# Turning q, k and the attention output with VectorE block transposes and a DRAM buffer instead of TensorE transposes

## The chip, the core and the metric

The kernel runs on one core of a Trainium2 chip. Five engines work side by side, each through its own list of instructions in order: TensorE (PE, matrix products into PSUM), VectorE (DVE), ScalarE (ACT), GpSimd (POOL) and SyncE (SP), which here issues nearly all the transfers between DRAM and the on-chip memory (SBUF). Sixteen DMA engines carry those transfers out. The metric is the device time of one execution in microseconds (us).

## What is computed

The inputs are q, k, v and o_gate of shape (4, 8, 768, 40) (batch, heads, steps, head size), two gates per step and head, and three weight matrices. First an attention with a matrix memory (an mLSTM), step by step for each batch and head:

```python
m_new = np.maximum(f_gate[:, :, t] + m, i_gate[:, :, t])
f_stab = np.exp(f_gate[:, :, t] + m - m_new)
i_stab = np.exp(i_gate[:, :, t] - m_new)
C = f_stab * C + i_stab * np.einsum('bhd,bhe->bhde', vt, kt)
n = f_stab * n + i_stab * kt
h_tilde = np.einsum('bhde,bhe->bhd', C, qt)
denom = np.maximum(np.abs(np.einsum('bhd,bhd->bh', n, qt)), 1.0)
y[:, :, t] = sigmoid(o_gate) * h_tilde / denom
```

Then a gated feed-forward layer over the 3072 tokens, whose input x is y with the heads side by side (320 columns):

```python
out = (sigmoid(x @ w_gate) * (x @ w_val)) @ w_out     # 320 -> 1536 -> 320
```

## The kernel before

**Chunks and units.** The 768 steps are cut into 6 chunks of 128. A unit is one chunk of one batch, so there are 24 units, n = 4 c + b. Within a unit the attention is computed as a matrix of scores (q times k, times a decay matrix d), times v, plus what the state C of the earlier chunks gives. The feed-forward layer (FFN) is cut into 103 steps: each takes one of the 12 slices of 128 hidden columns, for two batches of a chunk (256 tokens) or for all four (512 tokens).

**Names of the steps of a unit n** (a suffix .g is one of three groups of heads, 3, 3 and 2). lq, lk, lv, lo and ld load q, k, v, o_gate and the decay row. tr transposes q and k on TensorE through an identity matrix (line 638 from unit 8 on), six transposes in all. kh, kl and qk (lines 645, 650, 657) copy the result out of PSUM: kh is the part rounded to the format fp32r, kl the remainder, qk a full copy. From unit 8 on, sw (line 672) stores kh and kl into a DRAM buffer, six DMAs, and sr (lines 683 and 686) loads them back in another arrangement, four DMAs: three blocks of 40 rows on top of each other, so that one matmul with 120 rows (s, line 664, one per head) gives the sum of the high and low products. t multiplies the scores by d. da, db, va and vb split d and v, av (line 753) multiplies them, in and ti add the state's part, nd, ns and ro make the output x. xd copies 64 columns of it, xt (line 795) transposes it on TensorE in three pieces, xh and xl (lines 802 and 806) split it into high part and remainder for the FFN. cs, cd, cm and ca update the state. The units 0 to 7 use an older way for the scores, without the DRAM buffer (lines 599 to 629).

**Steps of an FFN step.** u0, u1 and r0, r1 are the products with w_gate and w_val (lines 863, 867, 868), th is the tanh on ScalarE, gx the product on VectorE, gh and gl the split on ScalarE and VectorE, dn (lines 897 to 899) the product with w_out, one per batch. ob stores a finished block of the output. The names that begin with w (wd, wa, wb, ...) load and split the weights.

**The order.** Nothing is planned at run time: a list of some 2,700 names, ORDER, is written out by hand or by a program, and the steps are issued in this order. Each engine thus gets its own instructions in that order and waits in place when an input isn't there; SP's list holds the transfers in the same way, so a transfer that waits holds back the later ones.

**Buffers.** The names in the first argument of sbt are tags: tiles with the same tag take turns in as many buffers as are given (one if none). The operands of the scores (tags bh and bl) have one buffer each, so a unit's sr waits for the last score matmul of the unit before. The PSUM tag pa has two buffers, in which tr, s, in, av, xt and cs take turns. The DRAM buffers are two, one for even and one for odd units.

Of the kernel before, what the change touches and what calls it, by code (L numbers as in the profile page):

```python
# [23 lines left out]
    'AV': 2,  # L24
    'K': [4, 12, 3, 0, 0, 12],
# [11 lines left out]
    i3 lf li wz lk0 i1 wm lq0 wdv0 i2 ga tap tr0.2 tr0.0 lo1 i0 lq1 gm0 sp1.0 cp0.0 cp0.2 sp0.0 i6 gb tac ee1.0  # L37
    tr0.1 sp0.1 i5 gc qb0.0 em1.0 gm1 gm2 gm3 cp0.1 ee0.0 em0.0 ee0.1 em0.1 lk1 tr1.1 tr1.0 wdr0 lk2 gs0 cp1.0 wav0
    war0 wdg0 cp1.1 sp1.1 qb0.2 s0.2 tr1.2 qb1.1 ee1.1 lv0 l10 qb1.0 dl0 t0.2 kw0 cp1.2 lq2 s0.0 qb0.1 wag0 s1.0
    qb1.2 wbv0 s0.1 ld2 t0.0 wbr0 em1.1 zs3 t0.1 wbg0 wcr0 og1 lo0 wcv0 wor0 dl1 lv1 wov0 s1.1 s1.2 wcg0 tr2.0 cp2.0  # L40
    l11 t1.2 whr0 t1.0 av0 lv3 whv0 wdo0 wdo1 og0 t1.1 ns0 cs0 ee2.1 wlr0 nd0 ro0 av1 wog0 cm0.0 wlv0 wao0 wao1
    tr2.1 wbo0 xd0 cp2.1 wbo1 wco1 qb2.1 whg0 nd1 wdv1 ns1 wco0 cm0.1 xt0 xh0 ro1 ld3 qb2.0 woo0 xd1 lq3 woo1 ee2.0
    xt1 xl0 wdg1 lo2 lo3 who0 wlg0 xh1 xl1 u0.0 gm4 gm5 r0.0 who1 ee3.1 wlo1 u1.0 th0 wdo2 kw1 r1.0 cs1 wlo0 wag1
    wbg1 og3 tr2.2 gs1 wao2 wdr1 lq5 lv2 wav1 l12 gx0 gh0 cm1.0 cm1.1 wcg1 zs1 gl0 wbv1 wog1 wbo2 gd whg1 em2 wco2
    lk3 ld4 dl2 kw2 u0.1 u1.1 tr3.0 wdg2 cp2.2 tr3.2 lv5 qb2.2 cp3.0 tr3.1 cp3.2 og2 cp3.1 qb3.0 wlg1 s2.1 s2.0 woo2
    who2 tab t2.1 r0.1 wlo2 war1 wag2 l13 zs0 t2.0 tbp tbc lk4 r1.1 dn0.1 qb3.1 wcv1 wbr1 zs2 th1 s2.2 t2.2 cs2
    cm2.1 cm2.0 av2 dn0.0 gx1 gh1 wov1 whv1 wlv1 qb3.2 lo6 wcr1 wbg2 tdp wor1 tdc wdo3 u0.2 ld5 wdv2 nd2 wao3 ns2
    tep gl1 dn1.1 s3.1 dn1.0 ro2 xd2 ee3.0 em3 wbo3 u1.2 wco3 whr1 dl3 wlr1 wdr2 woo3 who3 wlo3 tec t3.1 ee4.1 s3.2
# [140 lines left out]
def mlstm_then_gated_ffn_kernel(  # L189
# [101 lines left out]
    if PARAM["V32"] < NCH - 1:  # L291
# [659 lines left out]
```

## Time and profile before

| | |
|---|---|
| time, median of 3 runs | 557.59 us (554.11 to 567.98) |
| profiled execution | 555.66 us, of which 553.7 us are the span from the first to the last instruction |
| busy: TensorE, VectorE, ScalarE, GpSimd | 530.0, 328.0, 230.1, 246.8 us |
| DMA | 131644 packets, 72.34 MB |

In a row that describes a group of instructions stand the line, the engine, the operation, output<-input with sizes, the count, then after the bar the busy time in us and the mean of one in ns, then the idle time of the engine just before them and what ended it. Matmuls overlap, so a busy time summed over groups of TensorE counts the same moment more than once. Rows in order of time begin with the start and the length in us. Rows of transfers issued by SP (SPq) give the time that the issue takes, not the transfer.

### The profile page before, as it was taken

How to read it: one execution, taken by the hardware profiler on the slowest of the kernel's cores; microseconds unless marked ns; L12 is line 12 of the kernel's file. 1: busy time of each engine (PE TensorE's matmuls, PEld its weight loads, DVE VectorE, ACT ScalarE, POOL GpSimd, SP SyncE). 2: the span in 40 equal slices, each digit the busy share in tenths (PEclk: the TensorE clock that was granted, in tenths of full speed). 3: DMA queues.
4: the chain of work that ended last, by engine and by line, in shares of the span. 5: the costliest groups of instructions: out<-in, count | busy, mean ns of one | idle time of the engine just before them, and what ended most of it. 6: DMA issues, size and time to landing. Idle time of an engine off the chain costs nothing.

```text
span 553.7 us, 10954 instructions
## 1 busy us (share of the span) xinstructions
PE 530.0 (96%) x4101; PEld 485.6 (88%) x4101; DVE 328.0 (59%) x734; ACT 230.1 (42%) x580; POOL 246.8 (45%) x293
## 2 busy tenths in 40 slices
PE   7678999999989999999999999999999999999997
PEld 7567988879989899998889887988988888999997
DVE  5988877865655564764564654667543554543332
ACT  4767874663523433343342353233243232233322
POOL 3676646565444633337447381663701574300000
PEclk9879999999999999999999999999999999999999
DMA  9897573430787446277786537667047674010000
GB/s 205 228 234 211 135 225 73 134 106 22 179 194 184 125 113 126 58 178 203 171 200 120 114 118 161 177 168 181 25 133 154 147 183 115 27 26 25 25 1 24
DMA packets 131644, 72.34 MB, mean 131 GB/s; under 512 B 103112, under 2 KB 120776, under 8 KB 131592
## 3 DMA queue, kind: packets, MB, share of 16 engines
q1 hardware_dynamic: 130504, 71.39, 52.4%
q8 instruction: 32, 0.52, 0.4%
q10 hardware_dynamic: 1088, 0.26, 0.3%
q14 instruction: 20, 0.16, 0.1%
HBM read 56.95 MB, written 14.68 MB: 129 GB/s over the span
## 4 chain that ended last, share of the span: by engine, by line
PE 73%; DMA 9%; DVE 7%; ACT 4%; SPq 2%; issue 2%; POOL 1%; ACTq 0%; DVEq 0%; POOLq 0%
PE pg L863 28%; PE po L897 7%; PE po L899 6%; PE po L898 6%; PE pg L867 5%; PE pg L868 5%; PE av L753 4%; DMA qs<-scr 2%; PE s L664 2%; PE in L736 2%; PE pt L638 2%; PE cs L816 2%; DVE gl L887 1%; PE av L760 1%; PE xt L795 1%
## 5 line engine op out<-in xcount | busy, mean ns | idle before, releaser
L863 PE MATMUL pg<-xh,wh 128*128 128x256 f32 (+1 forms) x412 | 106.3, 340 | 2.0 <-ACT sg L873 1.4
L877 DVE SCALAR_TENSOR_TENSOR sg<-sg,pg 128x256 f32<-128x256 f32 (+1 forms) x103 | 54.1, 525 | 89.0 <-PE pg L868 72.9
L863 PE MATMUL pg<-xl,wh 128*128 128x256 f32 (+1 forms) x412 | 101.6, 328 | 0.0
L863 PE MATMUL pg<-xh,wl 128*128 128x256 f32 (+1 forms) x412 | 101.5, 328 | 0.0
L882 ACT ACTIVATE gh<-sg 128x256 fp32r<-128x256 f32 (+1 forms) x103 | 51.8, 502 | 107.2 <-DVE sg L877 80.8
L897 PE MATMUL po<-oh,gh 128*128 128x320 f32 x288 | 95.8, 332 | 0.0
L899 PE MATMUL po<-oh,gl 128*128 128x320 f32 x288 | 89.7, 311 | 1.0 <-DVE gl L887 1.0
L873 ACT ACTIVATE sg<-pg 128x256 f32<-128x256 f32 (+1 forms) x103 | 48.1, 467 | 101.1 <-PE pg L868 61.1
L898 PE MATMUL po<-ol,gh 128*128 128x320 f32 x288 | 89.2, 310 | 0.0
L887 DVE TENSOR_TENSOR gl<-sg,gh 128x256 fp32r<-128x256 f32 (+1 forms) x103 | 67.2, 652 | 36.5 <-ACT gh L882 36.1
L863 PEld LDWEIGHTS pg<-xl,wh 128*128 128x128 f32 x412 | 69.7, 191 | 7.2
L863 PEld LDWEIGHTS pg<-xh,wl 128*128 128x128 f32 x412 | 69.6, 190 | 7.2
L863 PEld LDWEIGHTS pg<-xh,wh 128*128 128x128 f32 x412 | 67.2, 191 | 5.3 <-ACT sg L873 2.3
L867 PE MATMUL pg<-xh,w 128*128 128x256 f32 (+1 forms) x206 | 70.4, 343 | 0.1
L868 PE MATMUL pg<-xl,w 128*128 128x256 f32 (+1 forms) x206 | 67.3, 328 | 0.0
L709 POOL TENSOR_TENSOR dr<-d 128x1024 f32<-128x1024 f32 x16 | 31.7, 1979 | 61.6 <-DVE d L693 61.4
L897 PEld LDWEIGHTS po<-oh,gh 128*128 128x128 f32 x288 | 54.5, 189 | 2.9
L898 PEld LDWEIGHTS po<-ol,gh 128*128 128x128 f32 x288 | 54.4, 189 | 2.9
L899 PEld LDWEIGHTS po<-oh,gl 128*128 128x128 f32 x288 | 54.2, 188 | 1.7 <-DVE gl L887 1.7
L693 DVE TENSOR_TENSOR d<-s,d 128x384 f32<-128x384 f32 (+1 forms) x72 | 35.5, 508 | 28.1 <-PE s L664 22.2
L593 POOL TENSOR_SCALAR_AFFINE_SELECT d<-d 128x1024 f32<-128x1024 f32 x22 | 25.8, 1175 | 45.7 <-ACT d L589 44.9
L585 POOL TENSOR_TENSOR d<-at,d 128x1024 f32<-128x1024 f32 x16 | 31.8, 1995 | 26.7 <-DMA d<-mscr 19.1
(143 smaller groups left out, 916.5 us busy)
## 6 DMA issues: line engine op xcount, KB each, us to landing
d<-mscr SPq DMA_DIRECT2D x22, 512.0 KB
ks<-scr SPq DMA_DIRECT2D x16, 360.0 KB
qs<-scr SPq DMA_DIRECT2D x16, 360.0 KB
k<-in_k_dram SPq DMA_DIRECT2D x24, 160.0 KB
o<-in_o_gate_dram SPq DMA_DIRECT2D x24, 160.0 KB
v<-in_v_dram SPq DMA_DIRECT2D x24, 160.0 KB
su_o<-in_moe_w_out_dram SPq DMA_DIRECT2D x12, 320.0 KB
out_dram<-ob SPq DMA_DIRECT2D x24, 160.0 KB
```

Source lines behind the costliest of these rows:

```text
L585: E("ea", n).tensor_tensor(dm[n], a, dm[n], ALU.subtract)
L693: nc.vector.tensor_tensor(y, ps_[n, g][:, :nh, :], y, ALU.mult)
L863: nc.tensor.matmul(p, w[y][:, a, fs], x[c][:, a, n0:n1], start=(i + a == 0), stop=False)
L867: nc.tensor.matmul(pg[n, y], w2[y][:, fs], xh[c][:, 2, n0:n1], start=False, stop=False)
L868: nc.tensor.matmul(pg[n, y], w2[y][:, fs], xl[c][:, 2, n0:n1], start=False, stop=True)
L873: nc.scalar.activation(s, pg[n, 0], AF.Tanh, scale=0.5)
L877: nc.vector.scalar_tensor_tensor(sgs[n], sgs[n], 1.0, pg[n, 1], ALU.add, ALU.mult)
L882: nc.scalar.activation(ghs[n][:, :nt], sgs[n], AF.Copy)
L887: E("gl", n).tensor_tensor(gls[n][:, :nt], sgs[n], ghs[n][:, :nt].bitcast(F32), ALU.subtract)
L897: nc.tensor.matmul(p, ghs[n][:, ts], oh[:, j, :], start=(j == 0), stop=False)
L898: nc.tensor.matmul(p, ghs[n][:, ts], ol[:, j, :], start=False, stop=False)
L899: nc.tensor.matmul(p, gls[n][:, ts], oh[:, j, :], start=False, stop=(j == NF - 1))
```

## The change

From chunk 2 on (units 8 to 23, the two new parameters QT and XT) there are no TensorE transposes of q, k and the output.

For q and k: tq turns 32 by 32 blocks of both on VectorE (two instructions, 320 columns each). tw writes the result to a DRAM buffer in runs of 32 numbers (128 bytes), in four DMAs, so that the buffer holds q and k with the head dimension as rows. sr loads it three times each for k and q, on rows 0, 42 and 84 (six DMAs, runs of 512 bytes; 42 rows each, of which 2 belong to the next head and are masked). sh on ScalarE rounds it to fp32r, with the sign turned in the one block that is to hold the remainder; sl on VectorE adds the full number there and nothing elsewhere, so that the operands hold high, remainder, high (k) and high, high, remainder (q), as before. The score matmuls have 126 rows instead of 120, one per head as before. sq loads the plain q for the state's part (two DMAs).

For the output: tx turns blocks on VectorE, xw writes them to DRAM (four DMAs), xr loads the turned output (three DMAs) into a buffer of tag dc, and xh and xl split it from there. xl moves from VectorE to GpSimd, and xd is dropped.

Two new set-up steps, i7 (the masks with signs) and i8 (zeros behind the DRAM buffers), replace zs0 to zs3. ORDER is replaced as a whole: 2,724 names for 2,710. Around the score matmuls of units 20 and 21 the new list reads:

```
... sl20.1 s20.1 s20.2 dn69.2 u0.71 gx70
dn68.0 og21 t20.1 s20.0 sr21.10 t20.0 u1.71 sr21.11 sr21.12 dn69.3 em21 gh70 r1.71 sq20.1 r0.71 gl70 sr21.00
sr21.02 sr21.01 dn69.0 dn70.0 dn70.3 t20.2 th71 gx71 lo22 l120 tq22 dn69.1 dn70.1 sh21.1 u1.72 dn70.2 r1.72
sl21.1 ld22 u0.72 da20 gh71 gl71 dn71.1 dn71.0 sh21.0 r0.72 lv22 th72 sl21.0 dn71.3 gx72 dn71.2 s21.1 s21.2 ...
```

The core of the diff:

```diff
+    'QT': 2,
+    'XT': 2,
...
+    DX = D + 2
+    scq = [dram.tile([2 * DM + 2, L], F32, name=f"scq{n}", tag=f"scq{n}") for n in range(2)]
+    scx = [dram.tile([DM, L], F32, name=f"scx{n}", tag=f"scx{n}") for n in range(2)]
+    rsign = const.tile([P, 6], F32, name="rsign")
...
+        def turned_out(name, dst, src):
+            dv = dst.rearrange("(n j) t -> j n t", j=32)
+            for a in range(4):
+                @op(f"{name}{n}.{a}")
+                def _(a=a):
+                    ts = slice(32 * a, 32 * a + 32)
+                    nc.sync.dma_start(dv[:, :, ts], src()[ts].rearrange("j (n i) -> j n i", i=32))
+
+        if bounced:
+            sc = scq[b % 2]
+
+            @op(f"tq{n}")
+            def _():
+                split[n] = t = sbt("kh", [P, 2, DM], F32, f"tq_{n}")
+                for x, y in enumerate((qt, kt)):
+                    nc.vector.transpose(t[:, x, :], y[n].rearrange("p h d -> p (h d)"))
+
+            turned_out("tw", sc[: 2 * DM], lambda: split[n].rearrange("p x d -> p (x d)"))
+
+            for x, y in ((1, "k"), (0, "q")):
+                for i in range(3):
+                    @op(f"sr{n}.{x}{i}")
+                    def _(x=x, y=y, i=i):
+                        if (n, x) not in stk:
+                            stk[n, x] = sbt("bl" if x == 0 else "bh", [P, 9, L], F32R, f"{y}s_{n}")[:, :H]
+                        src = sc[x * DM : x * DM + DM].rearrange("(h d) t -> d h t", d=D)
+                        src = bass.AP(tensor=src.tensor, offset=src.offset, ap=[[src.ap[0][0], DX]] + [list(z) for z in src.ap[1:]])
+                        nc.sync.dma_start(stk[n, x][i * DX : (i + 1) * DX].bitcast(F32), src)
+
+                @op(f"sh{n}.{x}")
+                def _(x=x, y=y):
+                    r = 3 * DX
+                    sgn[n, x] = t = sbt("st", [P, H, L], F32, f"{y}t_{n}", 3)
+                    nc.scalar.activation(t[:r].bitcast(F32R), stk[n, x][:r].bitcast(F32), AF.Copy, scale=rsign[:r, 5 - x : 6 - x])
+
+                @op(f"sl{n}.{x}")
+                def _(x=x):
+                    r = 3 * DX
+                    R = stk[n, x]
+                    nc.vector.scalar_tensor_tensor(R[:r], R[:r].bitcast(F32), rsign[:r, 3 - x : 4 - x], sgn[n, x][:r], ALU.mult, ALU.add)
+
+            for y in range(2):
+                @op(f"sq{n}.{y}")
+                def _(y=y):
+                    r = 3 * D
+                    if y == 0:
+                        qk[n] = sbt("qk", [P, 3, L], F32, f"qk_{n}", 2)
+                        nc.sync.dma_start(qk[n][:r, :2], sc[: 2 * r].rearrange("(g r) t -> r g t", r=r))
+                    else:
+                        nc.sync.dma_start(qk[n][: 2 * D, 2], sc[2 * r : DM])
+
+            for g, (h0, nh) in enumerate(GROUPS):
+                @op(f"s{n}.{g}")
+                def _(g=g, h0=h0, nh=nh):
+                    ps_[n, g] = p = pst("pa", [P, 3, L], f"s_{n}_{g}")
+                    for m in range(nh):
+                        nc.tensor.matmul(p[:, m, :], stk[n, 1][: 3 * DX, h0 + m, :], stk[n, 0][: 3 * DX, h0 + m, :], start=True, stop=True)
...
+        if xbounced:
+            sx = scx[b % 2]
+
+            @op(f"tx{n}")
+            def _():
+                tx[n] = sbt("kl", [P, DM], F32, f"tx_{n}")
+                nc.vector.transpose(tx[n], xin[n][:, :DM])
+
+            turned_out("xw", sx, lambda: tx[n])
+
+            for y in range(3):
+                @op(f"xr{n}.{y}")
+                def _(y=y):
+                    if n not in xf:
+                        xf[n] = sbt("dc", [P, 3, P], F32, f"xf_{n}", 3)
+                    if y == 0:
+                        nc.sync.dma_start(xf[n][:, :2], sx[: 2 * P].rearrange("(a p) t -> p a t", p=P))
+                    else:
+                        nc.sync.dma_start(xf[n][HP[y - 1], 2], sx[2 * P :])
...
-            nc.scalar.activation(xh[c][:, :, bs], px_[n], AF.Copy)
+            nc.scalar.activation(xh[c][:, :, bs], xf[n], AF.Copy)
...
-            nc.vector.tensor_tensor(xl[c][:, :, bs], px_[n], xh[c][:, :, bs].bitcast(F32), ALU.subtract)
+            (E("xl", n) if xbounced else nc.vector).tensor_tensor(xl[c][:, :, bs], xf[n], xh[c][:, :, bs].bitcast(F32), ALU.subtract)
```

More of the change, by code (lines that the diff above doesn't have):

```diff
@@ new lines @@
+    og15 s15.0 xr13.2 t15.2 sq15.1 s15.1 tw16.2 xw14.1 vb15 t15.0 t15.1 lk17 xr13.1 xl12 dn49.1 da15 xw14.2 gh51
+    gl51 r0.52 dn50.2 th52 av15.0 in15 ti15 dn50.3 tw16.3 dn50.0 db15 r1.52 dn51.3 xw14.3 dn50.1 av15.1 sr16.00
+    av15.2 dn51.0 gx52 gh52 lv16 l116 va16 xh13 ad15 ns15 nd15 ro15 u0.53 xr14.0 tx15 gl52 r0.53 xw15.0 sr16.02
+    xw15.1 u1.53 r1.53 dn52.0 sr16.01 dn51.1 tq17 xr14.1 kw15 xr14.2 xw15.2 tw17.0 xw15.3 dn51.2 th53 gx53 gh53
+    dn52.1 gl53 ea17 u0.54 xl13 xh14 r0.54 dn52.3 dn53.1 ee17 u1.54 r1.54 cs15 dn52.2 dn53.2 dn53.0 dn53.3 sr16.10
@@ L178 @@
+    gh100 gl100 th101 u0.102 r0.102 gx101 u1.102 gh101 gl101 r1.102 dn100.2 dn100.3 dn101.2 dn101.3 th102 gx102
+    gh102 gl102 dn102.3 dn102.2 ob5.3 ob5.2
 """.split()
@@ L334, in _ @@
                                 fill=0.0, base=-(L - 1), channel_multiplier=1)
+    if PARAM["QT"] < NCH:
+        @op("i7")
+        def _():
+            w = rsign[:, 1:4]
+            nc.gpsimd.memset(w, 1.0)
+            nc.gpsimd.affine_select(out=w, in_=w, pattern=[[-DX, 3]], compare_op=ALU.is_ge,
+                                    fill=0.0, base=0, channel_multiplier=1)
+            nc.gpsimd.affine_select(out=w, in_=w, pattern=[[DX, 3]], compare_op=ALU.is_ge,
+                                    fill=0.0, base=D - 1, channel_multiplier=-1)
+            m = rsign[:, 0:1]
+            nc.gpsimd.tensor_tensor(m, w[:, 0:1], w[:, 1:2], ALU.add)
+            nc.gpsimd.tensor_tensor(m, m, w[:, 2:3], ALU.add)
+            nc.gpsimd.tensor_scalar(rsign[:, 4:6], w[:, 1:3], -2.0, m, ALU.mult, ALU.add)
+        @op("i8")
+        def _():
+            for n in range(2):
+                nc.sync.dma_start(scq[n][2 * DM :], warm[:2, :L])
     @op("wm")
@@ L512, in unit @@
         halved = c >= PARAM["AV"]
+        bounced = c >= PARAM["QT"]
+        xbounced = c >= PARAM["XT"]
         spread = n < PARAM["BC"]
@@ L594, in _ @@
                                         fill=0.0, base=0, channel_multiplier=-1)
-        if not stacked:
+        def turned_out(name, dst, src):
[8 more added lines that the diff above has]
+            @op(f"tq{n}")
+            def _():
+                split[n] = t = sbt("kh", [P, 2, DM], F32, f"tq_{n}")
[36 more added lines that the diff above has]
+                        nc.tensor.matmul(p[:, m, :], stk[n, 1][: 3 * DX, h0 + m, :], stk[n, 0][: 3 * DX, h0 + m, :], start=True, stop=True)
+        elif not stacked:
@@ L785, in _ @@
                                      rden[n].unsqueeze(2).broadcast_to([P, H, D]), ALU.mult)
-        @op(f"xd{n}")
-        def _():
-            E("xd", n).tensor_copy(xin[n][:, DM:], xin[n][:, 2 * P : DM])
-        @op(f"xt{n}")
-        def _():
-            px_[n] = p = pst(P_(f"xt{n}"), [P, 3, L], f"xt_{n}")
-            for a in range(3):
-                nc.tensor.transpose(p[:, a, :], xin[n][:, a * P : (a + 1) * P], ident)
+        if xbounced:
+            sx = scx[b % 2]
+            @op(f"tx{n}")
+            def _():
+                tx[n] = sbt("kl", [P, DM], F32, f"tx_{n}")
[10 more added lines that the diff above has]
+                        nc.sync.dma_start(xf[n][HP[y - 1], 2], sx[2 * P :])
+        else:
+            @op(f"xd{n}")
+            def _():
+                E("xd", n).tensor_copy(xin[n][:, DM:], xin[n][:, 2 * P : DM])
+            @op(f"xt{n}")
+            def _():
+                xf[n] = px_[n] = p = pst(P_(f"xt{n}"), [P, 3, L], f"xt_{n}")
+                for a in range(3):
+                    nc.tensor.transpose(p[:, a, :], xin[n][:, a * P : (a + 1) * P], ident)
         @op(f"xh{n}")
```

277 lines of the change are left out of this document (134 added, 143 removed).

## The prediction, made before the change was run

> **What bounds the kernel now.** I read the page first: busy time by engine and the chain that ended last.
>
> ```profile
> PE 530.0 (96%) x4101; PEld 485.6 (88%) x4101; DVE 328.0 (59%) x734; ACT 230.1 (42%) x580; POOL 246.8 (45%) x293
> PE 73%; DMA 9%; DVE 7%; ACT 4%; SPq 2%; issue 2%; POOL 1%; ACTq 0%; DVEq 0%; POOLq 0%
> q1 hardware_dynamic: 130504, 71.39, 52.4%
> ```
>
> TensorE carries the end: 96% busy and 73% of the chain. A busy matmul can hide pipelining, so I asked next for busy time by stage (columns: stretch, length, busy us and instructions by engine, granted clock, DMA share, GB/s) and for TensorE's own waits from 120 us on.
>
> ```profile
> 0.00:56.00 56.00, 44.27 (x267) 37.36 (x268) 44.98 (x105) 36.05 (x105) 33.67 (x54) 0.91 0.91 220
> 56.00:140.00 84.00, 82.89 (x516) 73.28 (x514) 64.74 (x140) 50.39 (x130) 48.60 (x58) 1.00 0.43 116
> 140.00:480.00 340.00, 332.52 (x2735) 304.88 (x2735) 193.00 (x431) 121.61 (x291) 162.26 (x180) 1.00 0.59 143
> 480.00:553.60 73.60, 70.34 (x590) 70.06 (x588) 25.28 (x62) 22.01 (x55) 2.28 (x3) 0.99 0.07 21
> PE s L664 <- DMA qs<-scr: 2.9, 2, 1.8
> PEld s L664 <- issue: 3.5, 2, 2.0
> ```
>
> The change acts from 140 to 480 us. There TensorE is idle 7.5 us of 340, VectorE is busy 57%, ScalarE 36%, GpSimd 48%, and the DMA engines 59%. So work taken off TensorE comes off the time almost in full, provided that the new transfers arrive in time. The 11.7 us that TensorE idles in the first 56 us belong to loading and weight splitting, where DMA (91%) and VectorE (80%) are the full ones.
>
> **TensorE: what goes.** Per unit from 8 on (16 units), six transposes of q and k and three of the output. Their price is the distance between starts, not the 0.27 us that one lasts:
>
> ```profile
> 162.00 0.49 PE L795 MATMUL xt<-ident,x 128*128 128x128 f32 x3
> 162.33 0.27 PE L638 MATMUL pt<-ident,q 128*80 128x128 f32 x1
> ...
> 170.03 0.27 PE L638 MATMUL pt<-ident,q 128*120 128x128 f32 x1
> 170.14 0.27 PE L638 MATMUL pt<-ident,k 128*120 128x128 f32 x1
> 170.25 0.27 PE L638 MATMUL pt<-ident,q 128*120 128x128 f32 x1
> ```
>
> Three output transposes take 0.33 us, and each of the q and k ones 0.11. 16 x 9 x 0.11 = 15.8 us. The score matmuls keep their number and width (126 rows deep for 120), so they cost the same. Four of ten uses per unit of the two rotating PSUM buffers go too; I book nothing for that.
>
> **VectorE, ScalarE, GpSimd.** Rows for what goes and the nearest ones for what comes:
>
> ```profile
> L650 DVE TENSOR_TENSOR kl<-pt,kh 120x256 fp32r<-120x256 f32 x32 | 13.1, 416 | 3.0 <-ACT kh L645 3.0
> L650 DVE TENSOR_TENSOR kl<-pt,kh 80x256 fp32r<-80x256 f32 x16 | 6.6, 412 | 1.3 <-ACT kh L645 1.3
> L657 DVE COPY qk<-pt 120x128 f32<-120x128 f32 x32 | 9.1, 283 | 6.9 <-ACT kh L645 5.8 <-PE in L736 1.1
> L657 DVE COPY qk<-pt 80x128 f32<-80x128 f32 x16 | 4.5, 279 | 2.8 <-ACT kh L645 2.6
> L806 DVE TENSOR_TENSOR xl<-xt,xh 128x384 fp32r<-128x384 f32 x24 | 13.3, 555 | 13.2 <-ACT xh L802 13.1
> L617 DVE COPY qkt<-pt 120x256 f32<-120x256 f32 x7 | 2.9, 419 | 1.4 <-PE pt L606 1.3
> L887 DVE TENSOR_TENSOR gl<-sg,gh 128x256 fp32r<-128x256 f32 x62 | 34.8, 562 | 22.9 <-ACT gh L882 22.6
> L887 DVE TENSOR_TENSOR gl<-sg,gh 128x512 fp32r<-128x512 f32 x41 | 32.3, 788 | 13.6 <-ACT gh L882 13.5
> L645 ACT ACTIVATE kh<-pt 120x256 fp32r<-120x256 f32 x32 | 11.9, 380 | 17.9 <-PE pt L638 16.3 <-DMA scr<-kh 1.6
> L589 ACT ACTIVATE d<-d 128x1024 f32<-128x1024 f32 x16 | 16.8, 1053 | 0.0
> L484 POOL TENSOR_TENSOR ol<-dc_o,oh 128x320 fp32r<-128x320 f32 x12 | 12.3, 1024 | 7.3 <-ACT oh L479 5.6 <-DVE qbd L622 1.7
> L789 POOL COPY x<-x 128x64 f32<-128x64 f32 x23 | 8.4, 364 | 58.2 <-DVE x L784 58.2
> ```
>
> VectorE loses 13.1 + 6.6 + 9.1 + 4.5 + 16 x 0.555 = 42.2 us. It gains 32 sl at 1024 wide: by the slope of the gl rows (0.226 us per 256) 0.788 + 2 x 0.226 = 1.24 us, 39.7 us in all (up to 1.6 each at twice the 512-wide row); and 48 block transposes 320 wide. No transpose stands in the trace; by the copies' slope (0.136 us per 128) 0.49 us each, 23.5 us (between the 512-wide gl's 0.79 and the 128-wide copy's 0.28). Net +21 us, so 214 of some 324: 66%. ScalarE: 32 sh at the 1024-wide row's 1.053 = 33.7, less 48 kh at 0.38 = 18.2, net +15.5, to 42%. GpSimd: 16 xl from the 320-wide row scaled to 384, 1.23 each, less 16 xd at 0.364, net +14, to 54%. All three stay well under TensorE: nothing on the path. If that cover is gone, sl's 1.24 us stand whole ahead of gx and gl in VectorE's order, 1 to 2 us a unit.
>
> **DMA.** Per unit go 160 writes of 3072 bytes, 160 of 1024 and 720 reads of 1536. There come 3840 writes of 128 bytes (tw, xw) and 2720 reads of 512 (sr 2016, sq 320, xr 384). Prices per packet from stretches in which one kind runs alone: the v and k loads (160 bytes), and the last two stores (256 packets of 1280 bytes).
>
> ```profile
> 201.60:204.20 2.60, 2.60 (x24) 2.60 (x23) 1.67 (x5) 1.62 (x7) 0.89 (x3) 1.00 0.89 152
> 548.00:553.60 5.60, 2.34 (x16) 2.07 (x15) 1.14 (x3) 0.85 (x2) 0.00 (x0) 0.93 0.16 59
> 280.00:300.00 20.00, 19.41 (x197) 17.20 (x196) 10.07 (x24) 7.99 (x20) 11.57 (x17) 1.00 0.91 202
> ```
>
> 2.6 us x 0.89 x 16 engines over 395 KB of 160 bytes is 15.0 ns; 5.6 x 0.16 x 16 over 256 is 56 ns. The line through both gives 13.8 ns at 128 bytes, 28 at 512, 47 at 1024, 65 at 1536, 122 at 3072. Goes: 720 x 65 + 160 x 122 + 160 x 47 = 74 engine-us. Comes: 3840 x 13.8 + 2720 x 28 = 129. Net 55 per unit, 55 us of all 16 engines over the kernel; the stage goes from 0.59 x 340 = 201 to 256 us busy in 324, 79%. The run's own mean (52.4% x 553.7 x 16 / 130504 = 35.6 ns at 547 bytes, where the line says 29) would make it 83%. The fullest 20 us of the stage ran at 91%, so this still fits, with less room. Small writes to DRAM are not in the trace: their bounds are the semaphore-sized end of the line, 9 ns, and the 1280-byte store, 56; I take 13.8, being next to the 160-byte row.
>
> The Trainium skill, "DMA: Bandwidth & Descriptors", section Specifications, says that below 512 bytes the engine reads, modifies and writes. Taken as twice the price for the 128-byte writes, its sum is 556 (worked out from rows under the rivals). The 160-byte loads, at 15 ns, show no such step, but they write SBUF; no run here shows so small a write to DRAM.
>
> **Queues and waits.** SP's DMAs per unit go from 10 to 19, at 0.3 to 0.6 us each:
>
> ```profile
> 142.89 1.78 SPq L672 DMA_DIRECT2D scr<-kh  x3
> 150.03 0.33 SPq L683 DMA_DIRECT2D ks<-scr  x1
> 146.18 3.71 DMA scr<-kl
> 151.24 6.74 DMA qs<-scr
> ```
>
> That is 4 us more of a unit's 20 us. New waits on SP: tw on tq, sr on the landing of tw, xr on that of xw; behind them queue the loads of later units and the stores. On ScalarE, sh and xh now wait for transfers, with th and gh behind them; on VectorE sl, with gx and gl behind it.
>
> The tightest loop is the one pair of operand buffers (tags bl, bh): unit n's sr may start only when unit n-1's last score matmul has read them. Before, that was 4 issues (1.6 us) and the landing (6.7): 8.3 us, and the shortest TensorE work that the list put in between was 8.0 (unit 23), hence the 6.4 us of waits quoted first. Now it is 6 issues (2.5), the landing 6.7, one sh 1.05, one sl 1.24: 11.5 us. The work in between, counted in the new list with these prices from the chain:
>
> ```profile
> 256.81 1.40 PE pg L863 x6
> 342.37 0.15 PE po L898
> 343.83 0.23 PE pg L868
> ```
>
> Between the last score matmul of unit 20 and the first of unit 21 stand three u (1.40 each), four r (0.46), eleven dn (0.45): 11.0 us. The same count gives 10.4 for unit 23, 10.8, 11.1, 11.2 and 11.4 for units 17, 19, 22 and 10, and 13 or more elsewhere. Shortfall at 11.5: 3.1 us, where the old loop cost 2.9 as DMA waits: +0.2, and I put +1 for the longer ScalarE and VectorE queues in front of it. The distance from tq to the first score matmul is 25 to 41 us of TensorE work, against some 16 for tw, its 3.7 us landing and the rest: covered.
>
> **First 140 us.** The new list mixes units 2 to 6 earlier into the weight work. Up to u0.12 VectorE's instructions add up to 87 us of work in both lists, and TensorE's to 74 and 75: I book nothing, plus or minus 4. i7 (seven small GpSimd instructions) and i8 (two small stores) come in there, and the four zs stores go: nothing either, under the loading.
>
> **Sum**, against the profiled execution, 555.66 us (span 553.7 and 2.0 around it; the median of the runs shown, 557.59, lies 1.9 above): 555.7 - 15.8 + 1.2 = 541.
>
> **The rivals.**
> *The loop is longer than counted.* Up to four foreign issues stand among sr's six, 1.7 us, and sh may find ScalarE busy: at 14 us instead of 11.5 the shortfall of all units is 19, less the old waits of 2.9: 555.7 - 15.8 + 16 = 556. For it: gaps of 10.4 to 11.4 leave nothing. Against: the old list's shortest gap was equally close to its loop and cost 3.
> *DMA becomes the bound (slower).* Let a 128-byte write cost 2.5 times 13.8 ns, 35, near the run's mean packet. The stage then needs 256 + 1.5 x 53 = 336 us of all engines; at the best sustained share, 91%, it lasts 369 instead of 340: 585. It decides from twice the price on: there 256 + 53 = 309 us, at 91% 340, and the gain is just gone: 556. Against: bytes, not packets, fill most of this traffic, and the 160-byte packets cost 15. (Twice the price is what the rule of the Trainium skill named above would make of it.)
> *More than the transposes goes.* With fewer users of the rotating PSUM buffers the other waits of the stage go, and the first 56 us run better: 531.
>
> **How the numbers follow.** Forecast 53%, its own range 535 to 548; longer loop 17%; twice the price (556) 6%; DMA as the bound 19%; better still 5%. A run of this kernel can be told from no change at about 2%, 11 us: below 544.5 is faster, above 566.8 slower. Of the forecast's 53, 39 lie below 544.5: faster 0.44, same 0.37, slower 0.19. The range 532 to 572 leaves out the better end (4) and most of the DMA case (13).
>
> **What would show it.** Right: TensorE busy near 317 of 324 us in the stage, DMA share near 0.8, score matmuls waiting for sl a few us in all. The longer loop: those waits near 20 us, at units 10, 17, 19, 21 to 23. DMA as the bound: windows at 0.9 over the whole stage, landings far over 7 us, SP issues stretched to several us. Wrong in another way: ScalarE held by sh or xh with th behind it, or a first stage that ends more than 4 us later.

## The result and the profile after

The changed kernel takes 548.02 us (median of 4 runs, 545.87 to 549.6), the kernel before 555.85 us beside it (551.91 to 567.98): a ratio of 0.9865, 95% interval 0.9823 to 0.9907. The ratio leaves out executions in a slower state of the chip, so it isn't quite the quotient of the two medians. That is 1.35% less, between the forecast 541 and no change, and at the upper end of the forecast's own range (535 to 548). The profiled execution took 546.66 us (span 544.9), 9.0 us less than that of before, where the sum had 14.6.

The page of the kernel after: busy time by engine, the main DMA queue, the chain that ended last.

```profile
PE 518.4 (95%) x3957; PEld 472.7 (87%) x3957; DVE 360.5 (66%) x702; ACT 248.0 (46%) x564; POOL 266.2 (49%) x299
...
q1 hardware_dynamic: 221336, 73.20, 62.4%
...
PE 69%; DMA 13%; SPq 6%; DVE 5%; issue 3%; ACT 3%; POOL 1%; ACTq 0%; DVEq 0%; POOLq 0%
```

The 144 transposes are gone (4101 matmuls became 3957). VectorE has 32.5 us more work, ScalarE 17.9, GpSimd 19.4; in the chain, DMA and SP's issues take 19% where they took 11%. Busy time by stage of the kernel after, with the columns of the prediction:

```profile
0.00:56.00 56.00, 44.88 (x256) 36.64 (x257) 44.49 (x107) 36.83 (x109) 33.94 (x56) 0.88 0.85 209
56.00:140.00 84.00, 84.00 (x536) 75.70 (x534) 65.84 (x141) 50.33 (x128) 49.38 (x65) 1.00 0.59 147
140.00:480.00 340.00, 328.06 (x2653) 299.27 (x2652) 227.12 (x402) 141.77 (x280) 180.91 (x178) 0.99 0.71 143
480.00:545.00 65.00, 61.47 (x521) 61.10 (x519) 23.00 (x54) 19.07 (x48) 2.00 (x2) 1.00 0.09 25
```

From 140 to 480 us TensorE now idles 11.9 us instead of 7.5, and the granted clock is 0.99 instead of 1.00. Its own waits after 130 us (waiting line, what it waited for, us in all, times, longest):

```profile
PE pg L967 <- ACT sg L977: 5.6, 5, 2.1
PE s L679 <- issue: 2.8, 1, 2.8
PE s L679 <- PE pg L972: 1.8, 2, 1.0
PE s L679 <- DMA scq<-tq: 0.7, 1, 0.7
```

In the kernel before, the FFN's row (pg), from 120 us on, was:

```profile
PE pg L863 <- ACT sg L873: 1.4, 2, 0.9
```

After 130 us it is one wait of 0.9 us. So the row that grew most is not the score matmuls' (s) but the FFN's, which waited for the tanh (th, line 977). ScalarE's waits between 140 and 480 us show one thing that stood in front of th:

```profile
ACT qt L656 <- DMA qs<-scq: 9.1, 5, 3.9
ACT xh L906 <- DMA xf<-scx: 8.8, 4, 3.0
ACT kt L656 <- DMA ks<-scq: 8.5, 5, 2.9
```

Here ScalarE stands 26.4 us before sh (line 656) and xh (906), for operands that have not landed. The sum alone proves nothing, since before the change ScalarE stood still longer ahead of kh and xh:

```profile
ACT kh L645 <- PE pt L638: 25.5, 22, 3.0
ACT xh L802 <- PE xt L795: 23.7, 12, 5.0
```

But those waits were for TensorE, which was at work meanwhile. A wait for a landing can leave TensorE with nothing to do. The worst place, in order of time (start, length):

```profile
279.31 1.15 ACT L656 ACTIVATE qt<-qs,rsign 126x1024 fp32r<-126x1024 f32 x1 [3.88 <-DMA qs<-scq]
280.37 0.61 ACT L986 ACTIVATE gh<-sg 128x512 fp32r<-128x512 f32 x1
283.39 0.60 ACT L977 ACTIVATE sg<-pg 128x512 f32<-128x512 f32 x1 [2.41 <-DVE gl L991]
...
284.04 0.73 PE L967 MATMUL pg<-xh,wh 128*128 128x512 f32 x2 [2.15 <-ACT sg L977]
```

sh15.0 waits 3.88 us for its load; gh50, which is ready, stands behind it in ScalarE's order. gl50 then finds VectorE in sl15.0 (1.65 us) and two more steps, th51 waits for gl50 since the gate tile sg has one buffer, and TensorE idles 2.15 us. Two stretches around it (busy us by engine, then the granted clock):

```profile
282.00:285.40 3.40, 1.36 (x6) 1.14 (x7) 3.26 (x10) 2.01 (x3) 1.08 (x2) 1.00 0.89 195
285.40:288.80 3.40, 3.40 (x13) 2.79 (x12) 3.11 (x4) 1.52 (x7) 1.60 (x2) 0.51 0.11 41
```

After a stretch of 3.4 us in which TensorE was busy for 1.36 us its clock was granted at half for the next 3.4 us. Outside the first 40 us and the last 2 this never happened in the profiled execution of before.

**Where the gain went.** The end of FFN step 16's tanh came at 135.2 us before and at 134.8 after: the first stage neither gave nor took. From there to the last matmul I take off TensorE's gaps, and half of the time at half clock (matmuls 512 wide start 0.43 us apart there and 0.23 at full clock, so about half the work is lost); what is left is TensorE's own work. All columns are worked out from the traces' records, in us:

| kernel | stretch | gaps | half the time at half clock | left |
|---|---|---|---|---|
| before | 415.2 | 7.5 | 0 | 407.7 |
| after | 406.7 | 11.9 | 1.7 | 393.0 |
| e3, scores twice | 420.8 | 11.4 | 3.4 | 406.0 |
| e1, three moves | 410.8 | 12.8 | 6.8 | 391.2 |
| e2, more moves | 412.6 | 15.2 | 6.8 | 390.5 |
| e5, control of e6 to e8 | 406.0 | 11.0 | 1.7 | 393.2 |
| e6, two operand buffers | 404.4 | 8.4 | 5.1 | 390.8 |
| e7, two gate tiles | 409.5 | 13.1 | 3.4 | 393.0 |
| e8, both | 398.2 | 5.6 | 0 | 392.6 |
| e9, three operand buffers | 428.6 | 27.4 | 12.0 | 389.3 |
| e12, the same without added waits | 399.9 | 6.8 | 0 | 393.1 |

(A gap inside half clock is counted in both columns, so "left" comes out 2 to 4 us low where there is much of both.) TensorE's work fell by 14.7 us, close to the 15.8 booked. Of these, 4.5 went into more gaps and 1.7 into half clock; 0.4 came from the earlier start, and the sum, 8.9, is what the last matmul ends earlier by (541.47 against 550.34). Each row is one execution; those of e5, e8 and e12 are the fastest of their six.

### The profile page after: what moved, and what is told of

It is laid out like the page before. It is cut to its first block, busy times and chain, and to the rows that moved or that the text cites. A ratio compares the mean times of both kernels' runs of the same rounds, so it can differ in the third digit from the quotient of the medians.

```text
span 544.9 us, 10878 instructions
## 1 busy us (share of the span) xinstructions
PE 518.4 (95%) x3957; PEld 472.7 (87%) x3957; DVE 360.5 (66%) x702; ACT 248.0 (46%) x564; POOL 266.2 (49%) x299
## 3 DMA queue, kind: packets, MB, share of 16 engines
q1 hardware_dynamic: 221336, 73.20, 62.4%
## 4 chain that ended last, share of the span: by engine, by line
PE 69%; DMA 13%; SPq 6%; DVE 5%; issue 3%; ACT 3%; POOL 1%; ACTq 0%; DVEq 0%; POOLq 0%
PE pg L967 28%; PE po L1001 6%; PE po L1003 6%; PE po L1002 6%; PE pg L971 5%; PE pg L972 5%; DMA scx<-tx 3%; DMA qs<-scq 3%; PE av L837 2%; PE s L679 2%; DMA d<-mscr 2%; PE s L713 2%; PE av L844 2%; PE in L820 2%; SPq L650 1%
## 5 line engine op out<-in xcount | busy, mean ns | idle before, releaser
L991 DVE TENSOR_TENSOR gl<-sg,gh 128x256 fp32r<-128x256 f32 (+1 forms) x103 | 71.1, 690 | 40.1 <-ACT gh L986 39.8
L1001 PE MATMUL po<-oh,gh 128*128 128x320 f32 x288 | 92.3, 321 | 0.0
L967 PEld LDWEIGHTS pg<-xh,wh 128*128 128x128 f32 x412 | 67.9, 191 | 12.8 <-ACT sg L977 7.7
L971 PE MATMUL pg<-xh,w 128*128 128x256 f32 (+1 forms) x206 | 69.2, 338 | 0.0
L612 POOL TENSOR_TENSOR d<-at,d 128x1024 f32<-128x1024 f32 x16 | 33.0, 2068 | 21.8 <-DMA d<-mscr 17.4
```

Of the source, the lines that this page charges most:

```text
L612: E("ea", n).tensor_tensor(dm[n], a, dm[n], ALU.subtract)
L967: nc.tensor.matmul(p, w[y][:, a, fs], x[c][:, a, n0:n1], start=(i + a == 0), stop=False)
L971: nc.tensor.matmul(pg[n, y], w2[y][:, fs], xh[c][:, 2, n0:n1], start=False, stop=False)
L991: E("gl", n).tensor_tensor(gls[n][:, :nt], sgs[n], ghs[n][:, :nt].bitcast(F32), ALU.subtract)
L1001: nc.tensor.matmul(p, ghs[n][:, ts], oh[:, j, :], start=(j == 0), stop=False)
```

## The experiments

All ratios are to the kernel before, run on the same chip as the experiment. The theory at first (A): matmuls come off one for one, and what is missing went into a few places where a step that waits for a landing operand stands ahead of a step of the gate. Against it (B): the loss is spread, or the round trip through DRAM is the bound.

### e1 and e2: moves in the order list

e1 moves unit 7's denominator behind gl19 and the sign steps of units 13 and 15 behind th45, gl45 and th51. The last of the three:

```diff
-... th50 gx50 sh15.0 dn48.2 dn49.2 sl15.0 dn49.0 ... gl50 th51 lv15 sh15.1
+... th50 gx50 dn48.2 dn49.2 dn49.0 ... gl50 th51 sh15.0 sl15.0 lv15 sh15.1
```

> The changed kernel with three places of the order list mended, in chunks 3 and 4 of the list's first half: the denominator of unit 7 behind gl19, the sign steps sh13.0 and sl13.0 behind th45 and gl45, sh15.0 and sl15.0 behind th51; same instructions, same result. Theory A (the part of the transposes' 15.8 us that did not come off went into a few places where a landing operand's sign step, or a step on VectorE, stands ahead of a gate's step, so that TensorE waits for pg): the gaps of 1.5, 1.4 and 2.2 us at 153, 243 and 284 us go, and with the last of them the half clock that followed (1.7 us): 3 to 6 us less than the changed kernel, ratio to the kernel before about 0.977 to 0.981. Theory B (what is missing is spread: longer loops, slower VectorE steps, a lower granted clock whatever the order): each gap only moves to the next wait, less than 1.5 us comes off, ratio 0.984 to 0.989.

Measured: 548.88 us, ratio 0.9843 (0.9792 to 0.9894), not to be told from the changed kernel's 0.9865. Theory A's 3 to 6 us did not come. In the profile the gap at 243 us is gone and the one at 153 is down to 0.6, but unit 13's scores now wait 1.75 us at 248, and the gap at 284 came back as one of 4.05 us at 289, for gx51, with sl15.0 and the denominator of unit 14 ahead of it on VectorE.

e2 adds moves at units 22 and 23:

```diff
-... gl74 ... sh22.1 ro20 ... tx20 sl22.1 ... sh22.0 sl22.0 th75 gx75 ... t21.0 s22.1 t22.1 s22.0 ... u0.76 r0.76
+... gl74 ... th75 sh22.1 gh75 gx75 ro20 ... tx20 t21.0 sl22.1 ... sh22.0 gl75 sl22.0 ... u0.76 r0.76 u1.76 r1.76 s22.1 t22.1 s22.0
```

> As the run before, and further moves around units 22 and 23: t21.0 ahead of sl22.1, th75, gx75, gh75 and gl75 ahead of the sign steps of unit 22, the matmuls of u0.76 and u1.76 ahead of s22, th78 ahead of sh23.1; same instructions, same result. Theory A: TensorE's gap of 2.75 us ahead of s22 is filled with 2.8 us of matmuls that were ready, and part of the 0.85 us ahead of s23 too: another 2 to 3 us less than the run before, ratio about 0.972 to 0.977, with TensorE's idle time from 135 us on down from 11.9 to about 4 us. Theory B: less than 1 us beyond the run before.

Measured: 553.21 us, ratio 0.9911 (0.9878 to 0.9944): if anything, it took time. The gap ahead of s22 grew from 2.75 to 5.06 us. VectorE's steps there in the profile of e2:

```profile
445.15 0.69 DVE L984 SCALAR_TENSOR_TENSOR sg<-sg,pg 128x512 f32<-128x512 f32 x1 [4.37 <-ACT gh L989]
...
447.18 1.26 DVE L665 SCALAR_TENSOR_TENSOR ks<-ks,rsign,kt 126x1024 fp32r<-126x1024 f32 x1
448.36 2.38 DVE L994 TENSOR_TENSOR gl<-sg,gh 128x512 fp32r<-128x512 f32 x1
450.67 2.91 DVE L665 SCALAR_TENSOR_TENSOR qs<-qs,rsign,qt 126x1024 fp32r<-126x1024 f32 x1
```

The first row shows a slip of mine: gh75 came to stand ahead of gx75, so it rounds the tanh in place of the product (gl75, the difference to the product, makes up for it), and gx75 had to wait 4.37 us for it, with everything behind it on VectorE, sl22.1 too. So e2 does not test the move at unit 22 as it was meant. What it shows besides: gl75 and sl22.0 fell beside two GpSimd steps and took 2.38 and 2.91 us, where they need 0.68 and 1.28 alone (last section), and the idle stretch was followed by 10.2 us at half clock:

```profile
447.30:450.70 3.40, 1.32 (x6) 0.75 (x4) 3.40 (x3) 0.00 (x0) 3.29 (x2) 1.00 0.62 99
450.70:460.90 10.20, 7.21 (x70) 6.96 (x71) 6.72 (x12) 0.60 (x1) 4.20 (x3) 0.50 0.27 76
```

From e1, theory A as I had stated it falls: mending single places shifted the wait to the next step that was late. Whether a clean move at unit 22 would pay stays open. What the late steps share is the landing of the operands, and the next runs go there.

### e3: each score matmul twice

```diff
                         nc.tensor.matmul(p[:, m, :], stk[n, 1][: 3 * DX, h0 + m, :], stk[n, 0][: 3 * DX, h0 + m, :], start=True, stop=True)
+                        nc.tensor.matmul(p[:, m, :], stk[n, 1][: 3 * DX, h0 + m, :], stk[n, 0][: 3 * DX, h0 + m, :], start=True, stop=True)
```

> The changed kernel with each of the 128 stacked score matmuls issued twice into the same place: full result, 128 matmuls of TensorE more, no other work. Theory A (from the second stage on TensorE is the bound, and matmuls come off or on one for one): 128 x about 0.1 us = +12 to +13 us, near 560 us, ratio about 1.008; the operand wait of the next unit starts a microsecond later each time, so it may be 2 us more. Theory B (the operands' round trip through DRAM is the bound from unit 8 on): the second matmuls fall into the time in which TensorE waits and cost 0 to 4 us, ratio under 0.995.

Measured: 559.42 us, ratio 1.0037 (0.9998 to 1.0076), above the changed kernel's 0.9865 by 0.0172, 9.6 us of 557, give or take some 3; the profiled executions differ by 12.3. In the table TensorE's own work rises by 13.0 us, and the gaps hardly change. Theory A holds against theory B's 0 to 4 us: most or all of the added work shows in the time, so most of the 14.7 us that went off TensorE were really to be had.

### e4: each write of turned q and k twice

```diff
...
                     nc.sync.dma_start(dv[:, :, ts], src()[ts].rearrange("j (n i) -> j n i", i=32))
+                    if name == "tw":
+                        sv = spare[n % 2].rearrange("(n j) t -> j n t", j=32)
+                        nc.sync.dma_start(sv[:, :, ts], src()[ts].rearrange("j (n i) -> j n i", i=32))
```

> The changed kernel with each of the 64 writes of turned q and k (128-byte packets) issued a second time into a spare buffer in DRAM: full result, 40,960 packets and 64 issues on SP more. Theory A (DMA at 0.71 of the stage is not the bound): packets at 14 ns over 16 engines are 36 us of DMA time, which raise the share in the stage to about 0.8, and the time by 0 to 5 us, through later issues on SP; ratio 0.985 to 0.996. Theory B (128-byte packets and the queue are what holds the operands up): landings come 2 us later per unit or more, +15 to +36 us, ratio 1.01 to 1.05.

The four runs gave 552.8, 565.5, 566.2 and 568.3 us: too far apart for a ratio, 5 to 20 us above the changed kernel. The stretch from 135 to 540 us of the kernel after and then of e4 (its 566.2 us run), and e4's largest wait of TensorE:

```profile
135.00:540.00 405.00, 393.06 (x3198) 363.84 (x3197) 253.29 (x466) 163.12 (x333) 183.86 (x181) 1.00 0.62 125
```

```profile
135.00:540.00 405.00, 382.56 (x3044) 350.78 (x3042) 248.86 (x451) 156.56 (x317) 180.00 (x181) 0.97 0.69 137
```

```profile
PE pg L971 <- ACT sg L981: 10.8, 7, 2.4
```

The DMA engines are not full: a share of 0.69 with 40,960 packets more. Over the whole span the main queue took 33 us of all sixteen engines more than in the kernel after (66.1% of 564.4 us against 62.4% of 544.9), 13 ns a packet. The times decide nothing: one execution lies 4.8 us above the changed kernel, where theory A put it, and three lie 17 to 20 us above, where theory B put them. The profiled one is of the three; its longer stretch is gaps and half clock (22.4 and 10.2 us in the terms of the table, against 11.9 and 1.7). What the added writes cost by themselves, through packets or through the 64 more issues on SP, stays open.

### e5 to e8: more buffers

The buffers need room in SBUF. In these four kernels the tile of w_out's remainder is the tile of the rounded w_out itself, which therefore counts twice in the result; all instructions and the order stay (the remainder is still computed, into the tile of w_out it came from).

```diff
-    ol = const.tile([P, NF, DM], F32R, name="ol")
+    ol = oh
...
```

```diff
-stk[n, x] = sbt("bl" if x == 0 else "bh", [P, 9, L], F32R, f"{y}s_{n}")[:, :H]        # e6, e8
+stk[n, x] = sbt("bl" if x == 0 else "bh", [P, 9, L], F32R, f"{y}s_{n}", 2)[:, :H]
-sgs[n] = s = sbt("sg", [P, NT], F32, f"sg_{n}")[:, :nt]        # e7, e8
+sgs[n] = s = sbt("sg", [P, NT], F32, f"sg_{n}", 2)[:, :nt]
```

> The changed kernel with the remainder of w_out left out of the result (its tile is the rounded w_out itself), same instructions and order; it frees 15 KB per partition of SBUF and is the control for the next three. Both theories: as the changed kernel, ratio 0.983 to 0.990.

> The control (w_out's remainder left out) with two buffers each for the stacked operands of q and of k, so that SP issues the loads of the next unit without waiting for the last score matmul of this one. Theory A (the loop through the single operand buffers is what TensorE waits for ahead of s, 5.6 us of the changed kernel's 11.9 us of gaps, and what delays the sign steps ahead of th; every window of about 3.4 us with 1.8 us or more idle is followed by half clock, which costs 1.7 us or more): the operands land up to 10 us earlier, the gaps ahead of s fall under 1.5 us, no half clock between 50 and 540 us, 5 to 9 us less than the control, ratio 0.970 to 0.977. Theory B (the gate's chain on VectorE, slowed by GpSimd beside it, is what TensorE waits for, and the s gaps are only where that shows): the gaps move to pg, under 2 us less than the control.

> The control (w_out's remainder left out) with two buffers for the gate tile sg, so that th does not wait for gl of the step before. Theory A: the gaps of pg stay, since they come from sign steps that stand ahead of th and gh in the list; under 2 us less than the control. Theory B: the 5.7 us of gaps ahead of pg go, and the half clock with them: 4 to 7 us less than the control, ratio 0.974 to 0.980.

> The control (w_out's remainder left out) with both: two operand buffers and two gate tiles. If the two are separate causes, the gains of the two runs before add up: gaps from 135 us on near 2 us, no half clock in the middle, 8 to 12 us less than the control, ratio 0.965 to 0.972. If something third holds TensorE up (landing times on the DMA queues, the list itself), it is no better than the better of the two by more than 1.5 us.

| | median us | ratio | 95% interval |
|---|---|---|---|
| e5, control | 548.84 | 0.9837 | 0.9795 to 0.9879 |
| e6, two operand buffers | 542.99 | 0.9726 | 0.9683 to 0.9769 |
| e7, two gate tiles | 549.36 | 0.9846 | 0.9806 to 0.9886 |
| e8, both | 538.71 | 0.9662 | 0.9624 to 0.9701 |

The control stands where the changed kernel stands. Two operand buffers take 5.9 us off it, the size that theory A gave. Where the loop was tight it went as theory A said: SP issues the first load of k 18.8 and 20.0 us ahead of the first score matmul of units 21 and 22 (10.8 and 13.4 in the control), and the waits ahead of the scores of units 22 and 23 fell from 3.0 us to 0.4. But those of units 13 to 15 rose from 2.0 to 4.8; the longest, 2.8 us at unit 14, follows a sl14.0 that took 2.91 us beside a step of GpSimd (last section). So the gaps ahead of s are 5.3 us in all (5.1 in the control), those ahead of pg fell from 5.1 to 2.9, and the half clock that theory A excluded still came (10.2 us). The two traces explain only 3.2 us of the 5.9: the control's is the fastest of its six executions, e6's the second slowest. Two gate tiles alone give nothing, but together with two operand buffers they do: e8 is 10.1 us under the control, and its profile has no half clock between 40 us and the last matmul. TensorE's waits after 130 us, in e6 and then in e8:

```profile
PE s L679 <- issue: 3.6, 3, 2.8
PE pg L967 <- ACT sg L977: 2.8, 3, 1.5
PE s L679 <- ACT sg L977: 1.5, 1, 1.5
```

```profile
PE pg L967 <- DVE sg L981: 1.9, 1, 1.9
PE pg L967 <- ACT sg L977: 1.9, 3, 0.9
PE s L679 <- PE pg L972: 1.4, 2, 0.9
```

The three times fit this reading, which no run shows step by step: the late operands come first, and the gate's single tile passes on what is left of them. With both, 5.6 us of gaps remain, less than the 7.5 of before, and the stretch of the table is 17.0 us shorter than before: TensorE's work came off it in full.

### e9 to e11: the cure in the room that there is

e9 computes everything. Three buffers take turns for the two operands; tx goes to t1 and bmask into the second gate tile's place:

```diff
-stk[n, x] = sbt("bl" if x == 0 else "bh", [P, 9, L], F32R, f"{y}s_{n}")[:, :H]
+stk[n, x] = sb.tile([P, H, L], F32R, tag=turn3(), name=f"{y}s_{n}")     # bl0, bh0, kl0 in turn
...
-tx[n] = sbt("kl", [P, DM], F32, f"tx_{n}")
+tx[n] = sbt("t1", [P, DM], F32, f"tx_{n}", 2)
...
-sgs[n] = s = sbt("sg", [P, NT], F32, f"sg_{n}")[:, :nt]
+sgs[n] = s = sb.tile([P, NT], F32, tag=f"sg{n % 2 if n >= 24 else 0}", name=f"sg_{n}")[:, :nt]
...
-qt[n] = sbt("q", [P, H, D], F32, f"q_{n}", 3)
+qt[n] = sbt("q", [P, H, D], F32, f"q_{n}", 2)
```

> The full computation with both cures in the room that SBUF has: the stacked operands take turns in three buffers in place of two (the third is the tile that tx had; tx goes into t1), the gate tile has two buffers from step 24 on (the second in the place of bmask), q has two buffers in place of three, and seven loads of q stand later in the list for that. Theory A (two separate causes, each to be cured by a buffer, as the runs with more room had it: -1.1% and, both, -1.75%): with one operand of two loaded early, half to all of that: 4 to 9 us less than the changed kernel, ratio 0.968 to 0.977, gaps from 135 us on of 6 to 9 us. Theory B (the second operand still waits for the last score matmul, and both are needed): no gain from the operands, ratio 0.982 to 0.988.

Measured: 570.28 us, ratio 1.0215 (1.0179 to 1.0251), against both theories. The waits of TensorE, of SP (from 100 to 160 us) and of VectorE (from 200 to 250) in e9's profile:

```profile
PE po L1008 <- ACT gh L993: 10.4, 2, 9.9
PE av L844 <- DVE t L832: 5.9, 2, 4.2
```

```profile
SPq L657 <- PE s L720: 16.4, 1, 16.4
```

```profile
DVE t L832 <- DMA scx<-tx: 10.6, 2, 6.5
```

The buffer that my turn gave to unit 8 first was still held by unit 7. SP stood 16.4 us before that load, with the load of o_gate behind it, for which ScalarE waited 13 us ahead of gh. And ti waited for the DMA that reads tx out of t1. Two added waits cost more than the buffers gave.

e10 is e9 with e1's three moves.

> The run before with the three places of the order list mended as in the first run (unit 7's denominator behind gl19, the sign steps of units 13 and 15 behind th45 and th51). Theory A: with the operands early, the sign steps' places no longer decide; within 1.5 us of the run before. Theory B (in the first run the moves only shifted the wait onto operands that were late; with those early the moves are worth the gaps they remove): 2 to 4 us less than the run before.

Measured: 570.79 us, ratio 1.0209 (1.016 to 1.0259): as e9, and as theory A said, though under e9's own waits this says little.

e11 is e9 with xl on VectorE:

```diff
-        'gl': 'v', 'ca': 'v',
+        'gl': 'v', 'xl': 'v', 'ca': 'v',
```

> The kernel with three operand buffers and two gate tiles, and the 16 remainders xl of units 8 to 23 on VectorE (about 0.5 us each) in place of GpSimd (1.09 us each): VectorE takes 8 us more, GpSimd 17 us less. Theory C (GpSimd at work beside VectorE is what lengthens VectorE's steps: sl 1.28 us alone and 1.57 us beside it, gl 0.68 and 1.06 us): the other VectorE steps together take about 6 us less, and the time falls by 1 to 3 us. Theory D (GpSimd's remaining steps lie beside them all the same): VectorE's busy time rises by the whole 8 us, time unchanged or up to 3 us longer.

Measured: 578.58 us, ratio 1.0369 (1.0316 to 1.0422), 8.3 us more than e9. VectorE's busy time rises by 6.6 us, GpSimd's falls by 18.3. Two rows of its VectorE steps:

```profile
L917 DVE TENSOR_TENSOR xl<-xf,xh 128x384 fp32r<-128x384 f32 x16 | 11.3, 707 | 2.9 <-ACT xh L913 1.9 <-DMA scq<-tq 0.9
...
L998 DVE TENSOR_TENSOR gl<-sg,gh 128x512 fp32r<-128x512 f32 x41 | 39.8, 972 | 20.0 <-ACT gh L993 20.0
```

The other VectorE steps together take 4.7 us less (366.1 - 11.3 against 359.5), near the 6 of theory C; sl became 0.08 to 0.09 us shorter, but the 512-wide gl 0.10 longer (0.874 in e9). The time rose all the same, by more than theory D said: TensorE now waits 5.2 us for xl itself ahead of pg, and 3.5 us ahead of dn for gl, where e9 has 0.2.

### e12: the same cure without the added waits

```diff
+        return ("bh0", "bl0", "kl0")[n % 3]
...
+            if xbounced:
+                E("ro", n).tensor_tensor(ot[n], ot[n], rden[n].unsqueeze(2).broadcast_to([P, H, D]), ALU.mult)
+                return
...
-                tx[n] = sbt("kl", [P, DM], F32, f"tx_{n}")
+                tx[n] = sbt("x", [P, DM], F32, f"tx_{n}")
...
-            sgs[n] = s = sbt("sg", [P, NT], F32, f"sg_{n}")[:, :nt]
+            sgs[n] = s = sb.tile([P, NT], F32, tag="q2" if n >= 24 and n % 2 else "sg0", name=f"sg_{n}")[:, :nt]
```

The gate's second tile is the buffer that q gives up after unit 8.

> The full computation with the two cures as in the run of three operand buffers, but without that run's new waits (TensorE stood 9.9 us at 151 us, behind gh, while SP waited 16.4 us in the load of unit 8 for a score matmul of unit 7; and 4.2 us at 239 us, where VectorE's ti waited for the DMA that reads tx, now in t1): the stacked operands begin with the buffer that is free first (bh, then bl, then the former kl), tx lies in x, since the output is scaled in place, the masks bmask and cmask take no room, and q keeps three buffers until unit 8; four loads of q stand later in the list. Theory A (the two cures hold, the loss was the added waits): gaps from 135 us on of 6 to 10 us, at most one stretch of half clock in the middle, 2 to 8 us less than the changed kernel, ratio 0.970 to 0.983. Theory B (with three buffers the second operand still waits, so that only more room helps): ratio 0.984 to 0.990.

Measured: 543.31 us, ratio 0.9769 (0.9724 to 0.9815), whose interval lies wholly below the changed kernel's: the fastest kernel here that computes everything, 2.3% under the kernel before. Theory A holds, though the gain over the changed kernel, 0.0096 of the ratio, is about half of what e8 had under its control (0.0175). Its page's first row and TensorE's waits after 130 us:

```profile
PE 517.0 (96%) x3957; PEld 471.4 (88%) x3957; DVE 356.9 (66%) x702; ACT 247.3 (46%) x564; POOL 265.3 (49%) x296
```

```profile
PE pg L977 <- ACT sg L987: 1.9, 2, 1.6
PE s L686 <- issue: 1.4, 2, 0.9
PE pg L977 <- DVE sg L991: 1.1, 1, 1.1
```

The gaps are 6.8 us, and no half clock falls into the stretch of its profiled execution.

## Where the prediction held, and where it was off

**What goes off TensorE: right.** 15.8 us were booked; the traces give 14.7, and e3 gives 13.0 us for 128 matmuls (0.10 each). TensorE did bound the kernel: in e8, where the new waits are nearly gone, the stretch is shorter by the whole of the work that went.

**The other engines' work: direction right, size too small on VectorE.** +32.5 us against +21. Rows of the kernel after:

```profile
L662 DVE SCALAR_TENSOR_TENSOR ks<-ks,rsign,kt 126x1024 fp32r<-126x1024 f32 x16 | 23.9, 1491 | 6.9 <-ACT kt L656 5.6 <-DMA scq<-tq 1.2
L662 DVE SCALAR_TENSOR_TENSOR qs<-qs,rsign,qt 126x1024 fp32r<-126x1024 f32 x16 | 21.5, 1346 | 10.0 <-ACT qt L656 10.0
L877 DVE STREAM_TRANSPOSE tx<-x 128x320 f32<-128x320 f32 x16 | 8.1, 507 | 0.3
L991 DVE TENSOR_TENSOR gl<-sg,gh 128x512 fp32r<-128x512 f32 x41 | 36.9, 901 | 17.6 <-ACT gh L986 17.6
```

The transposes are at 0.49 to 0.51 us where the copies' slope gave 0.49. sl takes 1.35 to 1.49 us, not 1.24: the estimate holds for a sl alone (1.28 us) and not beside GpSimd (last section). The existing 512-wide gl went from 788 to 901 ns for the same reason, which the sum did not have. ScalarE's +17.9 and GpSimd's +19.4 were booked as 15.5 and 14.

**DMA: not the bound; the sum right, partly by luck.** The share of the stage is 0.71, not 0.79. Over the whole span the main queue took 50 us of all sixteen engines more (62.4% of 544.9 us against 52.4% of 553.7), where 55 were booked, but some 13 of them fell between 56 and 140 us (0.59 against 0.43). In the trace's packet records a 128-byte packet takes 14.0 ns on average, where the line gave 13.8. The larger ones were priced too low on both sides, and that cancelled: a 512-byte packet takes 38 ns, not 28, and the 1536-byte ones that went had taken 104, not 65. So the slower rival falls, at its own point of decision: the price of these writes did not double. The rule of the Trainium skill ("DMA: Bandwidth & Descriptors", Specifications: below 512 bytes read, modify, write), taken as twice the price, gave 556; the section names no price, and these writes of 128 bytes to DRAM show no doubled one. e4 adds that the engines have room.

**The loop: about as long as counted, set against an old cost that was misread.** From the last score matmul of one unit to the first of the next the trace has 11.4, 11.1, 11.6, 11.0 and 11.3 us at units 10, 17, 19, 21 and 23, where I counted a loop of 11.5, and 14.0 at unit 22, the size of the longer-loop rival. At units 10, 17 and 21 TensorE waits 0.1 us or less there, so these distances are its own work and show only that the loop isn't longer. The waits at the six units come to 3.9 us (2.75 at unit 22) for a counted 3.1. From this I took off 2.9 us as the cost of the old loop, and that was wrong: in the trace of before these two waits stand at unit 8 (1.76 us) and at unit 16 (1.11 us, 38 us after the scores of unit 15), and at unit 23, where the old loop was tight, TensorE doesn't wait. (The 6.4 us count these two waits twice, on the matmuls and on the weight loads.) Another 1.7 us stand at units 13 and 14, 16 us behind the unit before, where no shortfall was counted. In all, TensorE's gaps ahead of s grew from 3.4 us to 5.6, +2.2 for the +1.2 that stood for them.

**The term that was mis-sized: the new waits, +1.2 us.** They came to +4.5 us of gaps and 1.7 of half clock. I had counted only the loop that ends in s. The other way of a late operand was named under what would make the prediction wrong, but not priced: ScalarE held by sh or xh with th behind it. It came so: gaps ahead of pg rose from 0.9 to 5.7 us. e6 and e8 show that second buffers for the operands take most of this away (5.9 us, and 10.1 with the gate's second tile), and e1 that the three places in the list which looked guilty were not the cause. I priced neither the passing on through sg nor the clock.

**First 140 us: nothing, as booked** (134.8 against 135.2 us). The rival by which more than the transposes goes did not come: the other waits of the stage (cs, xt, po and the like) did fall, from 3.2 us to 0.5, but pg and s rose by more.

## What to carry to other kernels

When a result that was made on the spot begins to come through DRAM, price its lateness for every step that is queued behind the waiting one, on each engine, not only for the step that reads it. Before moving steps in a list that is full, ask which single buffer makes the transfer start late: a second buffer for it was worth 6 us where three moves in the list were worth nothing that could be measured. A new buffer order brings its own waits: look whether the first tile in turn is free, and what stands behind the transfer that waits for it.

## What the runs showed of the hardware

**TensorE's clock falls after half a window of idling.** The granted clock changes on a grid of 3.41 us. Over all profiled executions of this case there are 1550 windows of this grid between 130 and 520 us that began at full clock; 31 were followed by half clock. Every window with 1.81 us or more of TensorE idle was (25 of 25); between 1.49 and 1.80 us it was 6 of 14; below that, none. Half clock lasts 3.4 us, or 6.8 to 13.7 where gaps go on (10.2 in e2). So gaps that gather in one window cost 1.7 us beyond themselves, while the 7.5 us of before, spread over the stretch, drew no half clock. The Trainium skill ("TensorE: Matmul & The Clock Gate", Part 1: The HAM clock gate) has the window of about 3.4 us and gives an idle window as the condition; here about half of one was enough.

**VectorE steps with two tensors from SBUF grow beside GpSimd, transposes don't.** In the kernel after, sl takes 1.28 us where no GpSimd step overlaps it (17 of 32) and 1.57 on average where one does (up to 2.51); the 512-wide gl 0.68 (17 of 41) and 1.06 (up to 2.43). The transposes of q and k take 0.485 us either way, and gx, 512 wide with one input from PSUM, 0.68. It depends on the step of GpSimd too: where one step covered a sl or gl for over 0.8 of its length, in all runs with the change, xl made it 2.7 times as long on average (11 cases), while the masking of d on line 620 of the kernel after left it as it is (4 cases). The Trainium skill ("GPSIMD Engine Reference", Specifications) says that the two engines share SBUF interfaces, with contention for VectorE instructions with two SBUF inputs; these runs agree and give the price.
